# Gated scan and MoE on one core: another order of the head, h by units, and a table of shifted due times

## The chip, the cores and the metric

The program runs on one core of a Trainium2 chip. A core has five engines that run their own instruction queues in order and wait for each other through semaphores: TensorE (PE, matmuls), VectorE (DVE), ScalarE (ACT), GpSimd (POOL) and SyncE (SP, which here issues most of the DMA transfers). The metric is the device time of one execution in microseconds (us); lower is better.

## The reference

Two stages follow each other. The first is a gated linear recurrence over 768 tokens for 4 batches and 8 heads of 48 channels, the second a feed-forward layer over the 3072 tokens that come out of it.

```python
mag = np.sqrt(a_re * a_re + a_im * a_im)
scale = np.minimum(mag, 0.999) / (mag + 1e-06)
a_re_n, a_im_n = (a_re * scale, a_im * scale)
for t in range(S):
    ar, ai = (a_re_n[:, :, t, :, None], a_im_n[:, :, t, :, None])
    new_re = ar * S_re - ai * S_im
    new_im = ar * S_im + ai * S_re
    kv = np.einsum('bhd,bhe->bhde', k[:, :, t], v[:, :, t])
    S_re, S_im = (new_re + kv, new_im)
    y[:, :, t] = np.einsum('bhd,bhde->bhe', q[:, :, t], S_re)
...
h = x @ w_in                       # 3072x384 @ 384x2048
g = np.where(pos, h, np.where(neg, 0.0, (h + beta) ** 2 / (4.0 * beta)))
return (g @ w_out).astype(np.float32)   # 3072x2048 @ 2048x384
```

## The kernel before

The recurrence is computed without a loop over time. A complex gate is a decay and an angle; the running sums of both over the tokens turn the recurrence into masked attention between k and q that have been scaled by exponentials and by a sine and a cosine. The 3072 tokens are 12 units of 256 tokens. For each unit u, `gates(u)` makes the scaled k and q and `attend(u)` the attention:

- `gates(u)` first takes logarithms and exponentials of the gates (the first table of ACT, `natural_log_exp_and_others`), normalises, and for units 0 and 1 forms the running sum of the decay with matmuls against a triangular matrix (tile `o`, line 693). From that sum ACT makes two exponentials (line 747, into tile `x`), and DVE multiplies k and q (tile `kq`, one tile for both) by them (line 761). `yield` ends this part. The second part begins with a load of ACT's other table (`trig_and_small`, left out for unit 1, which shares unit 0's load), takes the arctangent, sums the angles with matmuls again, reduces them to turns (lines 773 and 781), takes sine and cosine (all plain ACT functions stand in line 644), and multiplies `kq` by each (`turn`, line 854: the product with the cosine goes into tile `x`, the one with the sine back into `kq`).
- `spread` moves these products into tiles `hd`, in which a head's 96 rows lie together: five DMAs for each product, ten for each unit, all issued by SP at line 434. In a packed tile `hd` the even rows come from one product and the odd rows from the other.
- `attend(u)` works on two chunks of 128 tokens. PE makes scores (line 1010) and transposes (950); DVE copies the scores under a causal mask (tile `am`, 1022), ACT copies the transposes (tile `kT`, 956); PE then adds the values (1054 with the state, 1062 with `am`) and the products for the state (979). The result goes to tile `xr`, and six small DMAs move the rest of its rows (`xr<-xr`).

`moe(blk)` is the feed-forward layer on a block of two units, 512 tokens, so there are six blocks. `split` casts `xr` to a rounded part `xH` (ACT) and the rest `xL` (DVE). For each of 16 slices f of the hidden layer `gemm1` accumulates nine matmuls of 512 columns into a PSUM tile `h` (there are two of them, in turn), ACT and DVE make g out of it (1212 to 1249; tile `g`, then its rounded part `gh` and the rest `gl`), and `gemm2` adds nine matmuls into three tiles `o` (line 1263) that last for the whole block. A tile `h` is free again when DVE has read it at line 1231. In block 0 two more steps of g are on ACT instead of DVE.

The weights are 16 packed loads (`raw_i`, `raw_o`). Each is decoded by three DVE instructions (464, 473, 482) and a cast on ACT (488) into `wi` or `wo`; its low part is made by PE and ACT for the first five loads (`rest`, 502, 503, 517) and by DVE (493) for the others. Slice f of the hidden layer needs loads `i` and `o` number f // 2.

Nothing is issued in the order in which it is written. Each operation goes into a `Plan` with an engine, a cost and what it depends on; `Plan.order` gives every operation a due time, backwards from the due times of the matmuls, and then schedules greedily: the engine that is free first takes the operation with the earliest due time among those whose inputs it takes to be ready. `emit` writes the instructions in that order and fills planned gaps of PE with idle matmuls (line 1326), up to the first matmul of `gemm1`. `NUDGE` is a table from the number of an operation to nanoseconds that are added to its due time.

Of the kernel before, what the change touches and what calls it, by code (L numbers as in the profile page):

```python
# [15 lines left out]
AF = mybir.ActivationFunctionType  # L16
# [3 lines left out]
P = 128  # L20
# [8 lines left out]
NJ = DM // P  # L29
NF = DFF // P  # L30
CH = 128
HC = CH // 2
U = 256
# [3 lines left out]
BLOCKS = ((0, 1), (2, 3), (4, 5), (6, 7), (8, 9), (10, 11))  # L37
# [25 lines left out]
MOVE_FIX, MOVE_ISSUE = 1750, 605  # L63
LOAD = 410.0
AHEAD, LATER, LATER_MOVE = 3000, 2000, 250
NUDGE = {}
MOVE = {16: 180, 32: 185, 128: 360, 288: 1330}
TABLE = 1294
FIRST = 66000
# [1 line left out]
LAG = 3  # L71
# [236 lines left out]
def per(n):  # L308
    return n / 2.4 + 14
# [23 lines left out]
def gated_scan_moe(  # L333
# [54 lines left out]
    pl = Plan()  # L388
# [28 lines left out]
    weight = {}  # L417
    seen = {}
    kinds = {}
# [7 lines left out]
    V_, A_, PE_ = nc.vector, nc.scalar, nc.tensor  # L427
# [15 lines left out]
    def table(name):  # L443
        pl.op("ACT", TABLE, lambda: nc.scalar.preload_act_table_set(name), w=[TAB])
# [160 lines left out]
    def gates(u):  # L605
# [32 lines left out]
        def ac(out, src, f, r, w, tab=False, **kw):  # L638
            acc_ = kw.get("accum_out")
            cost = act(N, ptr=not isinstance(kw.get("bias", 0.0), float), acc=acc_ is not None)  # L640
            (pl.op if acc_ is None else mark)(
                "ACT",
                cost,
                lambda: A_.activation(out(), src(), f, **kw),  # L644
                r=[*r] + ([TAB] if tab else []),
                w=w,
            )
# [31 lines left out]
        )  # L679
        js = ((0, 2), (2, 3))  # L680

        def running(src, part_, slots, name):

            out = []
            for (j0, j1), slot in zip(js, slots):
                R = tl(slot, [P, j1 - j0, U], F32, f"{name}_{u}_{j0}", ps)

                def run(R=R, j0=j0, j1=j1):
                    x = src().rearrange("p j t -> p (j t)")
                    for j in range(j0, j1):  # L690
                        for c in range(NC):
                            k = c * DM + j * P
                            PE_.matmul(
                                R.get()[:, j - j0, c * CH :],
                                x[:, k : k + P],
                                sums.rearrange("p c t -> p (c t)")[:, : U - c * CH],
                                start=c == 0,
                                stop=c == NC - 1,
                            )

                kinds[
                    pl.op("PE", (j1 - j0) * (pe32(U) + pe32(CH)), run, r=[part_], w=[R])
                ] = "sum"
                out.append(R)
            return out
# [55 lines left out]
        ve(dve(2 * N), lambda: V_.tensor_tensor(KQ.get(), KQ.get(), X.get(), op=ALU.mult), [X], [KQ])  # L761

        yield
        if u != 1:
            table("trig_and_small")
        ac(I, I, AF.Arctan, [], [i], True)
        c = 1.0 / (2 * math.pi)
        if by_token:
            for (j0, j1), R in zip(js, running(I, i, TOKEN[u], "turns")):
# [127 lines left out]
                        w=[(h, (e, 1 + q))],  # L897
                    )

        turn(X, 0)  # L900
        for g in range(3):
            spread(g, 0, X)
        turn(KQ, 1)
        for g in range(3):
            spread(g, 1, KQ)
        if u == 1:
            moved.append(len(pl.ops) - 1)

# [263 lines left out]
    def moe(blk):  # L1172
# [6 lines left out]

        def gemm1(f):  # L1180
            H = tl(turn_of("h", 2), [P, T], F32, f"h_{blk}_{f}", ps)
            for j in range(NJ):

                def mms(j=j):
                    sl = slice(j * P, (j + 1) * P)
                    for n, (part, x) in enumerate(((0, XH), (1, XH), (0, XL))):
                        PE_.matmul(  # L1187
                            H.get(),
                            weight["i", f // 2].get()[:, f % 2, part, sl],
                            x.get()[:, j, :],  # L1190
                            start=j == 0 and n == 0,
                            stop=j == NJ - 1 and n == 2,
                        )

                kinds[len(pl.ops)] = "moe"
                pl.op(
                    "PE",
                    3 * per(T),
                    mms,
                    r=[weight["i", f // 2]] + [(x, (ub, j)) for x in (XH, XL) for ub in range(len(BLOCKS[blk]))],  # L1200
                    w=[H],
                    due=t0 + STEP * (f + j / 6 - 0.6 * (f + 1 == NF and held_back > 0)),
                )
            SS = tl(turn_of("s", 3), [P, T], F32, f"s_{blk}_{f}")
            G = tl(turn_of("s", 3), [P, T], F32, f"g_{blk}_{f}")
            GH = tl(turn_of("gg", 6), [P, T], F32R, f"gh_{blk}_{f}")
            GL = tl(turn_of("gg", 6), [P, T], F32R, f"gl_{blk}_{f}")
            spare = blk < SPARE
            pl.op(
                "ACT",  # L1210
                act(T, ptr=True, psum=True),
                lambda: A_.activation(  # L1212
                    SS.get(), H.get(), AF.Relu, bias=c_half, scale=-0.5 if spare else 0.5
                ),
                r=[H],
                w=[SS],
            )
            if spare:
                pl.op(
                    "ACT",  # L1220
                    act(T, ptr=True),
                    lambda: A_.activation(SS.get(), SS.get(), AF.Relu, bias=c_one, scale=-1.0),
                    w=[SS],
                )
                pl.op(
                    "ACT", act(T), lambda: A_.activation(SS.get(), SS.get(), AF.Square), w=[SS]
                )
            pl.op(
                "DVE",
                dve(T),  # L1230
                lambda: V_.tensor_tensor(G.get(), H.get(), SS.get(), op=ALU.max),  # L1231
                r=[H, SS],
                w=[G],
            )
            if not spare:
                pl.op(
                    "DVE",
                    dve(T),
                    lambda: V_.scalar_tensor_tensor(  # L1239
                        G.get(), SS.get(), 1.0, G.get(), op0=ALU.min, op1=ALU.mult  # L1240
                    ),
                    r=[SS],
                    w=[G],
                )
            pl.op("ACT", act(T), lambda: A_.copy(GH.get(), G.get()), r=[G], w=[GH])  # L1245
            i = pl.op(
                "DVE",
                dve(T),
                lambda: V_.tensor_tensor(GL.get(), G.get(), GH.get().bitcast(F32), op=ALU.subtract),  # L1249
                r=[G, GH],  # L1250
                w=[GL],
            )
            gs[f] = (GH, GL)
            gated.append(i)
# [24 lines left out]

        held_back = BACK if blk == NBLK - 1 else 0  # L1280
        for k in range(NF + LAG):
            if k < NF:
                gemm1(k)
            if LAG <= k < NF + LAG - held_back:
                gemm2(k - LAG)
        for m in range(NJ if held_back else 0):
            for f in range(NF - held_back, NF):
                gemm2(f, (m,), NF - f - 1 + (m * held_back + f) / 9)
# [48 lines left out]
    first, second = gates(0), gates(1)  # L1337
    next(first)
    next(second)
    list(first)  # L1340
    attend(0)
    list(second)
# [300 lines left out]
```

## Time and profile before

| | |
|---|---|
| time, median of 3 runs | 573.28 us (572.74 to 575.54) |
| time of the profiled execution | 574.38 us |
| its span, first to last instruction | 572.6 us |
| PE busy | 558.9 us (98%), of it idle matmuls 27.3 us |
| DVE busy | 439.8 us (77%) |
| ACT busy | 391.2 us (68%) |
| granted TensorE clock, mean | 0.997 of full speed |

The profiled execution's time is 1.8 us longer than its span; that part lies around the first and the last instruction. The busy shares are means over the whole span, in which the first 76 us (gates and attention of units 0 and 1, the first weights, the first two slices) are another regime than the rest.

### The profile page before, as it was taken

The page shows a single profiled execution, that of the slowest core. Times are in us where ns is not written, and L with a number is a line of the kernel's source. Part 1 is how long each engine was busy: PE and PEld are TensorE (multiplying, and loading weights), DVE is VectorE, ACT ScalarE, POOL GpSimd, SP SyncE. Part 2 cuts the span into 40 slices and gives each one's busy share as a digit, 9 for nine tenths or more (in the row PEclk, how much of TensorE's full clock was granted, in tenths as well). Part 3 has the DMA queues.
Part 4 walks back from the last instruction along what each step waited for, and adds up shares of the span by engine and source line. Part 5 has one row for each costly group of instructions (what it writes and reads, how often), then busy time and mean ns, then how long its engine had stood idle before and what let it go on. Part 6 is the DMA issues. An engine that isn't in the chain of part 4 may idle for free.

```text
span 572.6 us, 10735 instructions
## 1 busy us (share of the span) xinstructions
PE 558.9 (98%) x4288; PEld 465.5 (81%) x4288; DVE 439.8 (77%) x611; ACT 391.2 (68%) x636; POOL 4.1 (1%) x27
## 2 busy tenths in 40 slices
PE   8999989999999999999999999999999999999996
PEld 8788868888888888888888888888888888888884
DVE  7998999989969988887797887987766555454562
ACT  7787688989975757757657686666455453369972
POOL 2000000000000000000000000000000000000000
PEclk9999999999999999999999999999999999999998
DMA  8848483663541512614403414402543500087811
GB/s 349 339 130 275 135 284 100 183 217 113 165 158 46 179 46 71 199 57 109 160 3 96 174 56 109 161 2 75 194 167 98 172 1 8 20 311 271 281 55 60
DMA packets 23686, 80.57 MB, mean 141 GB/s; under 512 B 4560, under 2 KB 10320, under 8 KB 23632
## 3 DMA queue, kind: packets, MB, share of 16 engines
q1 hardware_dynamic: 23488, 79.71, 42.1%
q8 instruction: 35, 0.57, 0.4%
q14 instruction: 19, 0.16, 0.1%
q10 hardware_dynamic: 144, 0.13, 0.1%
HBM read 55.05 MB, written 4.72 MB: 104 GB/s over the span
## 4 chain that ended last, share of the span: by engine, by line
PE 90%; DVE 3%; ACT 2%; DMA 2%; issue 1%; SPq 1%; POOL 0%; ACTq 0%; POOLq 0%; DVEq 0%
PE o L1263 35%; PE h L1187 34%; PE at L1010 6%; PE at L1062 3%; PE at L1054 3%; PE idle L1326 3%; PE at L979 3%; PE at L950 2%; DMA out_dram<-ob 1%; DVE kq L761 1%; ACT ai L644 1%; ACT x L747 1%; SPq L434 1%; DMA xr<-xr 1%; DVE ai L781 0%
## 5 line engine op out<-in xcount | busy, mean ns | idle before, releaser
L1187 PE MATMUL h<-xH,wi 128*128 128x512 f32 x576 | 181.3, 396 | 2.9 <-DVE g L1231 2.9
L1263 PE MATMUL o<-gh,wo 128*128 128x512 f32 x576 | 180.3, 394 | 0.0
L1187 PEld LDWEIGHTS h<-xH,wi 128*128 128x128 f32 x576 | 105.4, 188 | 25.0 <-DVE g L1231 3.5
L1263 PEld LDWEIGHTS o<-gh,wo 128*128 128x128 f32 x576 | 106.3, 188 | 22.8 <-issue 0.7
L1187 PE MATMUL h<-xL,wi 128*128 128x512 f32 x288 | 112.5, 391 | 0.4 <-DVE xL L1164 0.4
L1263 PE MATMUL o<-gl,wo 128*128 128x512 f32 x288 | 112.4, 390 | 0.0
L1231 DVE TENSOR_TENSOR g<-h,s 128x512 f32<-128x512 f32 x96 | 65.9, 687 | 54.4 <-ACT s L1212 53.6
L1212 ACT ACTIVATE s<-h,cst 128x512 f32<-128x512 f32 x96 | 65.8, 685 | 47.5 <-PE h L1187 46.6
L1245 ACT CAST gh<-g 128x512 fp32r<-128x512 f32 x96 | 59.3, 618 | 55.9 <-DVE g L1239 48.6
L1249 DVE TENSOR_TENSOR gl<-g,gh 128x512 fp32r<-128x512 f32 x96 | 65.8, 685 | 32.8 <-ACT gh L1245 30.8
L1187 PEld LDWEIGHTS h<-xL,wi 128*128 128x128 f32 x288 | 54.1, 188 | 12.7 <-DVE xL L1164 1.2
L1263 PEld LDWEIGHTS o<-gl,wo 128*128 128x128 f32 x288 | 54.1, 188 | 11.8 <-DVE gl L1249 0.3
L1239 DVE SCALAR_TENSOR_TENSOR g<-s,g 128x512 f32<-128x512 f32 x80 | 55.3, 691 | 2.2
L644 ACT ACTIVATE ai<-ai 128x768 f32<-128x768 f32 x48 | 40.4, 845 | 10.1 <-DVE ai L797 5.3
L1010 PEld LDWEIGHTS at<-hd 96*64 96x64 f32 x704 | 32.5, 137 | 7.6 <-issue 5.9
L1010 PE MATMUL at<-hd 96*64 96x64 f32 (+1 forms) x704 | 36.7, 251 | 0.0
L1022 DVE COPY_PREDICATED am<-tri,at 128x512 f32<-128x512 uint32 x44 | 32.1, 743 | 5.1 <-PE at L1010 4.2
L719 DVE TENSOR_TENSOR_SCAN ai<-again,ai 128x768 f32<-128x768 uint8 x20 | 35.1, 1753 | 0.4
L1062 PE MATMUL at<-am,V 128*64 128x128 f32 x352 | 32.9, 273 | 0.0
L1054 PE MATMUL at<-hd,st 96*64 96x128 f32 x304 | 30.5, 278 | 0.0
L1326 PE MATMUL idle<-tri,ident 128*128 128x128 f32 x208 | 27.3, 291 | 1.8 <-POOL tri masks.py:66 1.8
L1326 PEld LDWEIGHTS idle<-tri,ident 128*128 128x128 f32 x208 | 26.5, 206 | 2.8 <-POOL tri masks.py:66 1.8
(127 smaller groups left out, 642.5 us busy)
## 6 DMA issues: line engine op xcount, KB each, us to landing
chk<-in_wl_dram SPq DMA_DIRECT2D x16, 768.0 KB, 6.5
kq<-in_kq_dram SPq DMA_DIRECT2D x12, 768.0 KB, 6.0
ai<-in_ari_dram SPq DMA_DIRECT2D x10, 768.0 KB, 6.7
V<-in_v_dram SPq DMA_DIRECT2D x12, 576.0 KB, 4.1
hd<-x SPq DMA_DIRECT2D x24, 288.0 KB, 3.2
hd<-kq SPq DMA_DIRECT2D x24, 288.0 KB, 4.3
raw_i<-in_wl_dram SPq DMA_DIRECT2D x8, 768.0 KB, 6.9
raw_o<-in_wl_dram SPq DMA_DIRECT2D x8, 768.0 KB, 5.0
```

The source lines that it names most:

```text
L644: lambda: A_.activation(out(), src(), f, **kw),
L1010: PE_.matmul(SC.get()[o : o + HC, i + e, HC * k :], t[:, 0, ks], t[:, 1, qs], start=True, stop=True,)
L1054: PE_.matmul(o_, st.get().rearrange("p h e -> p (h e)")[:, lo : lo + 64], head(h)[:, 1, cs], start=True, stop=False,)
L1062: PE_.matmul(o_, V.get()[:, c, lo : lo + 64], ams[pr // 2].get()[:, 2 * (pr % 2) + e, :], start=st is None, stop=True,)
L1187: PE_.matmul(H.get(), weight["i", f // 2].get()[:, f % 2, part, sl], x.get()[:, j, :], start=j == 0 and n == 0, stop=j == NJ - 1 and n == 2,)
L1212: lambda: A_.activation(SS.get(), H.get(), AF.Relu, bias=c_half, scale=-0.5 if spare else 0.5),
L1231: lambda: V_.tensor_tensor(G.get(), H.get(), SS.get(), op=ALU.max),
L1239: lambda: V_.scalar_tensor_tensor(G.get(), SS.get(), 1.0, G.get(), op0=ALU.min, op1=ALU.mult),
L1245: pl.op("ACT", act(T), lambda: A_.copy(GH.get(), G.get()), r=[G], w=[GH])
L1249: lambda: V_.tensor_tensor(GL.get(), G.get(), GH.get().bitcast(F32), op=ALU.subtract),
L1263: PE_.matmul(PO[m].get(), weight["o", f // 2].get()[:, f % 2, part, sl], g.get(), start=f == 0 and n == 0, stop=f == NF - 1 and n == 2,)
L1326: PE_.matmul(idle["h1"], ident, mask, start=True, stop=True)
```

## The change

Five edits. (1) The generators of the two first units are advanced by turns: unit 0 up to its second table, then a load of that table, the arctangents of both units, a load of the first table for unit 1's exponentials, and a load of the second table again for the sines. (2) For units 0 and 1 the product with the sine comes first and goes into tile `x`, and the one with the cosine goes back into `kq`; for the other units nothing changes here. (3) In block 0 the slices f = 0 and 1 of `gemm1` run as two sets of nine matmuls with 256 columns, one for each unit. (4) `gemm2` is written ahead of `gemm1` of the same step. (5) `NUDGE` gets 195 entries.

```diff
-NUDGE = {}
+NUDGE = {
+    25: -59700, 43: 11500, 46: -22300, 58: -180800, 68: -10500, 74: -12000, 75: -16200,
...
+}
+HALVES = 2
...
+        def arctan():
+            ac(I, I, AF.Arctan, [], [i], True)
+
+        yield
+        if u == 1:
+            arctan()
+            yield
...
         yield
+        if u > 1:
+            table("trig_and_small")
         if u != 1:
-            table("trig_and_small")
-        ac(I, I, AF.Arctan, [], [i], True)
+            arctan()
+            yield
...
-        turn(X, 0)
-        for g in range(3):
-            spread(g, 0, X)
-        turn(KQ, 1)
-        for g in range(3):
-            spread(g, 1, KQ)
+        for t, e in ((X, 1), (KQ, 0)) if by_token else ((X, 0), (KQ, 1)):
+            turn(t, e)
+            for g in range(3):
+                spread(g, e, t)
...
         def gemm1(f):
             H = tl(turn_of("h", 2), [P, T], F32, f"h_{blk}_{f}", ps)
...
+            halves = blk == 0 and f < HALVES
+            for n, (lo, hi) in enumerate(((0, U), (U, T)) if halves else ((0, T),)):
+                ubs = (n,) if halves else range(len(BLOCKS[blk]))
+                for j in range(NJ):
...
+                    done = pl.op(
+                        "PE",
+                        3 * per(hi - lo),
+                        mms,
+                        after=[done] if n and not j else (),
+                        r=[weight["i", f // 2]] + [(x, (ub, j)) for x in (XH, XL) for ub in ubs],
+                        w=[(H, n)],
+                        due=t0 + STEP * (f + j / 6 - 0.6 * (f + 1 == NF and held_back > 0)),
+                    )
...
         for k in range(NF + LAG):
+            if LAG <= k < NF + LAG - held_back:
+                gemm2(k - LAG)
             if k < NF:
                 gemm1(k)
-            if LAG <= k < NF + LAG - held_back:
-                gemm2(k - LAG)
...
     next(first)
     next(second)
+    next(first)
+    table("trig_and_small")
+    next(first)
+    next(second)
+    table("natural_log_exp_and_others")
+    next(second)
+    table("trig_and_small")
     list(first)
```

What this does to the order shows at three places. ACT before, from the exponentials of unit 1's running sum (`x_156<-o`; unit 0's tiles are `ai_132` and `x_151`, unit 1's `ai_134` and `x_156`) over the table load and the two arctangents (`ai_132<-ai_132`, `ai_134<-ai_134`) to unit 0's sine, the first of the last row's two instructions:

```order
L747 ACTIVATE x_156<-o_112 128x2x256 x2
L747 ACTIVATE x_156<-o_113 128x256 x2
L517 CAST wi_252<-rest_i_0_257 128x384
L444 ACT_TABLE_LOAD
L517 CAST wi_252<-rest_i_1_272 128x384
L644 ACTIVATE ai_132<-ai_132 128x768
L644 ACTIVATE ai_134<-ai_134 128x768
L488 CAST wo_292<-raw_o_143 128x2x384
L488 CAST wi_304<-raw_i_147 128x2x384
L517 CAST wo_292<-rest_o_0_301 128x384
L644 ACTIVATE ai_132<-ai_132 128x768 x2
```

The same stretch of ACT in the changed kernel (unit 1's tiles are now `ai_135` and `x_161`), from the last exponentials of unit 0 to the sine, `ai_132<-ai_132` behind the third load, and the two casts after it:

```order
L674 ACTIVATE x_161<-x_161,cst 128x3x256
L785 ACTIVATE x_151<-o_113 128x256
L474 ACT_TABLE_LOAD
L674 ACTIVATE ai_132<-ai_132 128x768
L674 ACTIVATE ai_135<-ai_135 128x768
L474 ACT_TABLE_LOAD
L785 ACTIVATE x_161<-o_112 128x2x256 x2
L785 ACTIVATE x_161<-o_113 128x256 x2
L474 ACT_TABLE_LOAD
L674 ACTIVATE ai_132<-ai_132 128x768
L518 CAST wi_291<-raw_i_137 128x2x384
L518 CAST wi_294<-raw_i_139 128x2x384
```

The casts of weights have moved behind the sine, and three loads of a table stand there instead of one. On SP, before, the ten moves of unit 0 stand in this order, cosine product `x` and sine product `kq` in turns, with two loads of weights just ahead:

```order
L449 DMA raw_o_248<-in_wl_dram 128x1536
L449 DMA raw_i_276<-in_wl_dram 128x1536
L434 DMA hd_0_346<-x_151 48x1536
L434 DMA hd_1_349<-x_151 48x1536
L434 DMA hd_2_353<-x_151 32x1024
L434 DMA hd_0_346<-kq_139 48x1536
L434 DMA hd_1_349<-kq_139 48x1536
L434 DMA hd_2_353<-kq_139 32x1024
L434 DMA hd_2_353<-x_151 16x512 x2
L434 DMA hd_2_353<-kq_139 16x512 x2
```

And on SP in the changed kernel, where `x` is the sine product:

```order
L479 DMA raw_i_157<-in_wl_dram 128x1536
L464 DMA hd_1_306<-x_151 48x1536
L464 DMA hd_0_316<-x_151 48x1536
L464 DMA hd_2_321<-x_151 32x1024
L464 DMA hd_2_321<-x_151 16x512 x2
L464 DMA hd_0_316<-kq_141 48x1536
L464 DMA hd_1_306<-kq_141 48x1536
L464 DMA hd_2_321<-kq_141 32x1024
L464 DMA hd_2_321<-kq_141 16x512 x2
```

All five moves of `x` are now ahead of those of `kq`, and the two last loads of weights have gone behind all twenty moves of both units. The third place is DVE from the first g of block 0 (`g_0`) on, before:

```order
L1231 TENSOR_TENSOR g_0_801<-h_0_749,s_0_785 128x512
L665 SCALAR_TENSOR_TENSOR x_727<-ai_525,x_727 128x3x256
L1249 TENSOR_TENSOR gl_0_822<-g_0_801,gh_0_808 128x512
L1231 TENSOR_TENSOR g_1_834<-h_1_757,s_1_794 128x512
L1022 COPY_PREDICATED am_82<-tri,at_109 128x512
L493 TENSOR_TENSOR wi_824<-raw_i_492,wi_824 128x2x384
```

And after it:

```order
L1273 TENSOR_TENSOR g_0_774<-h_0_716,s_0_757 128x512
L503 SCALAR_TENSOR_TENSOR raw_o_711<-raw_o_711,y_o_770 128x768
L1273 TENSOR_TENSOR g_1_787<-h_1_690,s_1_762 128x512
L1291 TENSOR_TENSOR gl_0_792<-g_0_774,gh_0_783 128x512
L512 SCALAR_TENSOR_TENSOR raw_o_711<-raw_o_711 128x768
L1291 TENSOR_TENSOR gl_1_808<-g_1_787,gh_1_797 128x512
```

Decoding of weights that stood ahead of `g_0` now stands behind it. From `g_0` to block 0's last `gl` DVE has 104 instructions before and 109 after: seven of weights (two of line 473, two of 482, one each of 464, the low part of an `i` and of an `o`) and one of the state (line 991) have come in, and three of `xL` have gone behind. On PE, idle matmuls fall from 104 to 77, and behind the first matmul of `h` the stretches of feed-forward matmuls are broken by attention 51 times instead of 56.

## Rows read from the trace of the kernel before

**Rows 1.** Stretches of PE: us, busy (instructions), granted clock, DMA share, GB/s.

```profile
76.03:567.00 490.97, 490.75 (x3600) 1.00 0.38 125
...
569.70:570.00 0.30, 0.00 (x0) 0.50 0.19 34
```

**Rows 2.** Timeline of PE: start, us, line, tiles, count, idle before and its releaser.

```profile
34.01 6.86 PE L1326 MATMUL idle<-tri,ident 128*128 128x128 f32 x60
...
41.80 1.72 PE L1010 MATMUL at<-hd 96*64 96x128 f32 x32
...
76.03 0.74 PE L1187 MATMUL h<-xH,wi 128*128 128x512 f32 x2 [2.73 <-DVE g L1231]
```

**Rows 3.** Timeline of ACT: unit 0's first exponential, the table load, unit 0's sine.

```profile
15.61 0.60 ACT L747 ACTIVATE x<-o 128x512 f32<-128x512 f32 x1 [0.83 <-PE o L693]
...
21.37 1.28 ACT L444 ACT_TABLE_LOAD   x1
22.67 0.48 ACT L517 CAST wi<-rest_i 128x384 fp32r<-128x384 f32 x1
...
28.70 1.72 ACT L644 ACTIVATE ai<-ai 128x768 f32<-128x768 f32 x2 [0.50 <-DVE ai L781]
```

**Rows 4.** Groups of ACT from 13 to 34 us, columns as on the page.

```profile
L644 ACT ACTIVATE ai<-ai 128x768 f32<-128x768 f32 x6 | 5.0, 844 | 1.3 <-DVE state L806 0.6 <-DVE ai L781 0.5
...
L747 ACT ACTIVATE x<-o 128x512 f32<-128x512 f32 x4 | 2.3, 596 | 1.1 <-PE o L693 0.8 <-DVE state L736 0.2
L747 ACT ACTIVATE x<-o 128x256 f32<-128x256 f32 x4 | 1.4, 386 | 0.5 <-DVE state L736 0.5
```

**Rows 5.** Timeline of DVE in block 0: a low part, a decoding step, two `xL`.

```profile
128.47 0.95 DVE L493 TENSOR_TENSOR wo<-raw_o,wo 128x768 fp32r<-128x768 f32 x1
129.34 0.55 DVE L464 TENSOR_SCALAR y_i<-raw_i 128x768 uint32<-128x768 uint32 x1
129.81 0.68 DVE L1231 TENSOR_TENSOR g<-h,s 128x512 f32<-128x512 f32 x1
...
156.18 0.75 DVE L1164 TENSOR_TENSOR xL<-xr,xH 128x256 fp32r<-128x256 f32 x2
156.85 0.68 DVE L1249 TENSOR_TENSOR gl<-g,gh 128x512 fp32r<-128x512 f32 x1
```

**Rows 6.** Timeline of DVE in the head: a product, the first mask copy, a wait.

```profile
31.68 1.76 DVE L854 TENSOR_TENSOR x<-kq,ai 128x1536 f32<-128x1536 f32 x1
...
43.68 1.34 DVE L1022 COPY_PREDICATED am<-tri,at 128x512 f32<-128x512 uint32 x2
...
53.97 0.56 DVE L464 TENSOR_SCALAR y_o<-raw_o 128x768 uint32<-128x768 uint32 x1 [2.09 <-DMA raw_o<-in_wl_dram]
```

**Rows 7.** Timeline of SP: issues of unit 0's first moves.

```profile
33.47 1.86 SPq L434 DMA_DIRECT2D hd<-x  x3
35.43 2.21 SPq L434 DMA_DIRECT2D hd<-kq  x3
```

**Rows 8.** DMA issues from 35.4 to 37.65 and 33 to 35.4: KB, us to landing.

```profile
hd<-kq SPq DMA_DIRECT2D x2, 288.0 KB, 5.6
...
hd<-x SPq DMA_DIRECT2D x2, 288.0 KB, 3.7
```

**Rows 9.** Stretches of DVE, columns as in the first group: from the first mask copy, from g_0.

```profile
43.68:75.97 32.29, 29.27 (x40) 1.00 0.67 205
75.97:157.45 81.48, 77.71 (x105) 1.00 0.55 175
```

**Rows 10.** Timeline of PE: the first matmuls behind scores, and block 0's end.

```profile
131.11 0.73 PE L1187 MATMUL h<-xH,wi 128*128 128x512 f32 x2
131.68 0.39 PE L1187 MATMUL h<-xL,wi 128*128 128x512 f32 x1
...
157.35 0.62 PE L1263 MATMUL o<-gh,wo 128*128 128x512 f32 x2
157.81 0.39 PE L1263 MATMUL o<-gl,wo 128*128 128x512 f32 x1
```

More of the change, by code (lines that the diff above doesn't have):

```diff
@@ L1181, in gemm1, with mms @@
             H = tl(turn_of("h", 2), [P, T], F32, f"h_{blk}_{f}", ps)
[L1182 to L1203, printed above, removed]
+            halves = blk == 0 and f < HALVES
+            for n, (lo, hi) in enumerate(((0, U), (U, T)) if halves else ((0, T),)):
+                ubs = (n,) if halves else range(len(BLOCKS[blk]))
+                for j in range(NJ):
+                    def mms(j=j, lo=lo, hi=hi):
+                        sl = slice(j * P, (j + 1) * P)
+                        for n, (part, x) in enumerate(((0, XH), (1, XH), (0, XL))):
+                            PE_.matmul(
+                                H.get()[:, lo:hi],
+                                weight["i", f // 2].get()[:, f % 2, part, sl],
+                                x.get()[:, j, lo:hi],
+                                start=j == 0 and n == 0,
+                                stop=j == NJ - 1 and n == 2,
+                            )
+                    kinds[len(pl.ops)] = "moe"
+                    done = pl.op(
[6 more added lines that the diff above has]
+                        due=t0 + STEP * (f + j / 6 - 0.6 * (f + 1 == NF and held_back > 0)),
+                    )
             SS = tl(turn_of("s", 3), [P, T], F32, f"s_{blk}_{f}")
```

27 rows, old and new, of the table NUDGE are left out of this document.

## The prediction

> **What bounds the kernel now.** I read the page first, then stretches of PE, then the timelines of the first 76 us engine by engine, then DVE's stretches. The table above says that PE is busy for 98% of the span; the reader should see where that is useful work. From the third slice of block 0 at 76.03 us to the last matmul PE has 490.75 busy of 490.97 us [rows 1]: it is the limit there, and its time changes only if its instructions change or if something begins to make it wait. Ahead of that point PE is filled with idle matmuls, 6.86 us of them before unit 0's scores, and it waits 2.73 us before that third slice for DVE's g_0, which frees the PSUM tile [rows 2]. So the end is set by when g_0 is done, just ahead of 76.03, by PE's 491 us behind it, and by an unchanged tail of 5.6 us (572.6 less 567.0).
>
> **The head, step by step.** Unit 0's exponentials start at 15.61 us, and its sine at 28.70, when DVE has the turns [rows 3]. In the new order ACT first makes unit 0's four exponentials with one of unit 1 in between. The start moves little, since unit 0's chain is only placed ahead of unit 1's: I take 15.2. Two exponentials of 0.6 us, two of 0.4 and a plain function of 0.84 [rows 4] make 2.8 us; with a short wait for DVE's copy, 18.1. A table load takes 1.3 us from its start to the next instruction [rows 3]. So load, two arctangents (1.7), load, unit 1's four exponentials (2.0) and load end at 25.7. DVE has less ahead of unit 0's turns: one weight (three instructions, 0.5 + 0.9 + 0.9 from start to start), the last third of another [rows 5], and one product of 1.76 [rows 6], 5 us in all. Not all of it helps, because DVE must wait for the exponentials to scale k and q; adding up its queue in the new order from 15.2 on gives the turns at 25.7 too. The sine then starts at 25.8, 2.9 us sooner. The first product no longer waits for the cosine but for the sine, and follows it by 3.2 us (one plain function, DVE's product, two hand-overs): SP's first issue goes from 33.47 [rows 7] to 29.0. Behind the sine two casts of weights of the same 768 columns (1.7) and the absolute value stand ahead of the cosine, which ends at about 30.6; the second product ends at 32.4. These casts cost nothing as long as SP still issues `x`: three issues take 1.86 us [rows 7], so five last to 32.1. If they were longer they would move the second product one for one.
>
> The scores start 6.4 us after the second product's first issue now (35.43 to 41.80), with 5.6 us from issue to landing while `x` is still in flight, against 3.7 us for the first moves [rows 2, 7, 8]. In the new order `x` has had 3.4 us alone, so I take 4.8 us, between 4.3 (3.7 and one more issue) and 6.2 (5.6 and one more): scores at 37.2 instead of 41.80. The first mask copy, 1.9 us behind the scores' start, is at 39.2 instead of 43.68 [rows 6], 4.5 us sooner, 3.1 to 5.0 by these ends. From there to the end of g_0 at 75.97 DVE needs the same work in both orders, 29.27 us, and loses 3.02 us [rows 9], of which 2.09 on a load of weights [rows 6]; that load is now issued right behind the moves, some 6 us sooner. I give back half of that wait: g_0 ends at 70.4, **5.5 us sooner**; with none of it back and late landing 3.1, with all of it and early landing 7.1.
>
> The halves of slices 0 and 1 are inside that number. Eighteen matmuls of 256 columns move into the wait for unit 1's moves, where idle matmuls stood; the other eighteen replace eighteen of 512 columns at 0.23 us [rows 10]. Half the columns cost from 0.12 us (half the time) to 0.23 us (no gain) each, so 2.1 to 4.1 us instead of 4.1. Either way it is over before g_0, which hangs on DVE's queue; without that cover it would be worth up to 2 us.
>
> **PE's own work behind it.** Where feed-forward matmuls follow scores, the first two take 0.57 us from start to start instead of 0.46 [rows 10]. I price every change from the one kind to the other at these 0.11 us. With 51 stretches instead of 56, two changes into attention and five out of it are gone: **0.8 us less**. Nothing to twice that are the ends, since the row shows two matmuls and not what lies around them.
>
> **What DVE is owed.** The work that leaves the head comes back. Between g_0 and block 0's last `gl` DVE has seven weight instructions and one state update more and three `xL` less. From start to start a long weight instruction takes 0.87 us, a short one 0.47 (the state update I take as a short one), two `xL` of 256 columns 0.67 and one of 768 as long as a low part of that size [rows 5]: 6 x 0.87 + 0.47 + 0.47 - 0.67 - 0.87 = 4.6 us more. This stretch is 81.48 us with 77.71 busy [rows 9], that is 3.8 us lost to waits, and PE reaches that `gl` only 0.3 us after it is made (157.81 against 156.85 + 0.68) [rows 5, 10]. PE's work in between is the same. So PE must wait 4.6 - 3.8 - 0.3 = 0.5 us plus whatever DVE still loses: 0.5 us if it never waits, 4.3 us if it loses as much as now. The new order interleaves DVE's chains more, so I take 1.7 us lost: **2.2 us given back**. Further on it costs nothing more: DVE's share falls and each slice's g is made many us ahead.
>
> The other edits have one answer: writing `gemm2` ahead of `gemm1` and the due times act only through the order counted above, and the tail's order is the same from slice 12 of the last block on.
>
> **Sum.** -5.5 - 0.8 + 2.2 = -4.1 us against the profiled execution's own 574.38 us, which is 1.1 us above the median shown: 570.3 on its scale, 569.2 us on the median's.
>
> **A rule against the change.** By the rows a switch of table costs 1.3 us, and the cast behind it starts at once [rows 3]; the two added loads are 2.6 us of ACT, in the chain above. The Trainium skill, "ScalarE: Activation LUTs", section "What ACT_TABLE_LOAD costs", puts a switch at about 2.66 us, a load of 1.28 us and a drain of about the same length, and its rules for kernel authors ask to do all of one set before switching. By that the two added loads would cost 5.3 us and the gain of the head would be some 2.7 us less; the trace has the load's length as stated and no drain behind it, so I go by the trace.
>
> **The rivals**, each on the median's scale. *DVE's debt is paid in full.* DVE loses 3.8 us in block 0 as now, so PE waits 4.3 us: -5.5 - 0.8 + 4.3 = -2.0, 571.3 us. For it: DVE stands at 95% there. Against it: its waits were harmless so far and nothing ordered them away. *TensorE's clock falls.* The granted clock is at half (0.50, the 1.2 GHz level) in the stretch from 569.70 us, 2.7 us after the last matmul, but at 1.0 through the stretches that follow the 2.73 us wait before 76.03 [rows 1, 2]. In the new order only ten idle instructions (five idle matmuls), 1.1 us by the sixty of 6.86, stand between the last work at about 32.2 and the scores at 37.2, a wait of some 4 us. If the clock falls there, unit 0's first scores and values, 4 to 5 us of PE, take up to 2.3 us more, and the gain shrinks to 1.8: 571.5 us. The skill's page "TensorE: Matmul & The Clock Gate" says in its part 1 that the throttled clock is the default and that only activity releases it, which speaks for this. *Nothing moves.* Scores wait for something other than the moves, as a weight's cast: the head gains nothing, but work has also not left DVE's early queue: about 573 us. *Slower.* DVE becomes the limit of block 0: each us that it loses there beyond 1.7 is a us of PE, so from 5.8 us lost (0.5 + 5.8 eats the 6.3) the kernel is no faster, and from 8.7 us it is slower by 0.5%. The head shows that DVE can lose 2.09 us to one load, but block 0 loses 3.8 in all now; at 10 us it would be 577.5 us. *Better.* Early landing, all of the 2.09 us back and DVE almost without waits: -7.1 - 0.8 + 0.8 = -7.1, 566.2 us.
>
> **How the numbers follow.** A difference under 0.5% (2.9 us) can't be told from none in these measurements. Forecast, 567.4 to 570.6: 0.45. Better than that: 0.21. DVE's debt or the clock, 570.6 to 573: 0.23. Nothing: 0.04. Slower than before: 0.07, most of it by over 0.5%. Faster by over 0.5% holds the forecast, the better case and a small part of the rivals' low ends: 0.68. Same: 0.26. Slower by over 0.5%: 0.06. The range leaves out one in ten at each end: 565.0 to 572.6 us.
>
> **What would show it.** In the profile after: unit 0's sine at 25 to 26.5 us; the first `hd<-x` issue near 29 and the scores near 37; g_0 done near 70.5; PE waits for DVE in block 0 (on `g`, `gl` or a weight) of about 2 us in sum, where there were none; no waits behind it; table loads with no gap behind them. The forecast is wrong if scores start after 39, if the clock falls before them, or if PE's waits in block 0 pass 4 us.

## The result, and the profile after

| | before | changed |
|---|---|---|
| time, median of 8 runs each | 574.85 us (572.74 to 576.82) | 569.68 us (567.77 to 571.05) |
| ratio | | 0.991, 95% interval 0.989 to 0.994 |
| time and span of the profiled execution | 574.38, 572.6 us | 570.26, 568.5 us |
| mean granted clock of the profiled execution | 0.997 | 0.992 |

The kernel is 0.9% faster; 0.7% (569.2 against 573.28 us) was forecast. By the medians that is 5.2 us. Between the two profiled executions the difference is 4.1 us, as the sum had it, but it is put together in another way.

The stretches of PE in the changed kernel, from the end of slice 1 of block 0 (us, busy and instructions, granted clock, DMA share, GB/s):

```profile
65.90:69.24 3.34, 0.00 (x0) 0.75 0.86 255
69.24:74.50 5.26, 5.26 (x13) 0.51 0.60 150
74.50:563.00 488.50, 488.03 (x3589) 1.00 0.39 128
```

Against [rows 1] PE's work from slice 2 on begins 6.8 us sooner (69.24 for 76.03) and ends only 4.0 sooner. The reason stands in the middle line: the granted clock, which was 1.0 through the wait before 76.03, falls within the wait before 69.24 (0.75 in the mean there) and is at half, the 1.2 GHz level, for nearly all of the next 5.26 us. The timeline of PE shows the same from the matmuls (line 1048 makes scores, 1228 is `gemm1`, 1305 `gemm2` in the changed kernel):

```profile
36.45 1.56 PE L1048 MATMUL at<-hd 96*64 96x128 f32 x32
...
69.24 1.22 PE L1228 MATMUL h<-xH,wi 128*128 128x512 f32 x2 [3.35 <-DVE g L1273]
70.26 0.63 PE L1228 MATMUL h<-xL,wi 128*128 128x512 f32 x1
...
74.49 0.63 PE L1305 MATMUL o<-gh,wo 128*128 128x512 f32 x2
...
151.94 0.50 PE L1305 MATMUL o<-gh,wo 128*128 128x512 f32 x1 [0.15 <-DVE wo L523]
154.81 0.50 PE L1305 MATMUL o<-gl,wo 128*128 128x512 f32 x1 [0.27 <-DVE gl L1291]
```

The wait for g_0 is still there and has grown from 2.73 [rows 2] to 3.35 us. Behind it twelve matmuls last from 69.24 to 74.49, 5.25 us, where twelve cost 12 x 0.23 = 2.8 at [rows 10]. The two waits for DVE in block 0 are 0.4 us together as listed. Of the head, ACT's timeline from unit 0's first exponential to its sine:

```profile
14.64 1.08 ACT L785 ACTIVATE x<-o 128x512 f32<-128x512 f32 x2 [1.21 <-PE o L731]
...
17.51 1.28 ACT L474 ACT_TABLE_LOAD   x1
18.81 1.58 ACT L674 ACTIVATE ai<-ai 128x768 f32<-128x768 f32 x2
20.41 1.28 ACT L474 ACT_TABLE_LOAD   x1
21.70 1.83 ACT L785 ACTIVATE x<-o 128x512 f32<-128x512 f32 x4
23.55 1.28 ACT L474 ACT_TABLE_LOAD   x1
24.89 0.84 ACT L674 ACTIVATE ai<-ai 128x768 f32<-128x768 f32 x1
```

Each of the three loads takes 1.3 us from its start to the next instruction, as in [rows 3]. (The Trainium skill, "ScalarE: Activation LUTs", section "What ACT_TABLE_LOAD costs", has a drain of about the length of a load with each switch; none of the three shows one.) SP's moves of unit 0 follow:

```profile
28.15 3.31 SPq L464 DMA_DIRECT2D hd<-x  x5
31.56 3.21 SPq L464 DMA_DIRECT2D hd<-kq  x5
```

And DVE, in stretches from the first mask copy to g_0 and from g_0 to block 0's last `gl`:

```profile
37.65:69.19 31.54, 29.31 (x41) 0.97 0.66 219
69.19:154.76 85.57, 81.69 (x110) 0.97 0.53 173
```

The first line answers to 32.29 us with 29.27 busy [rows 9]: the same work, 0.8 us less lost. The second has 4.0 us more work than [rows 9] and loses 3.9 us, as much as before. Where it loses them DVE's timeline tells:

```profile
75.63 0.69 DVE L1273 TENSOR_TENSOR g<-h,s 128x512 f32<-128x512 f32 x1 [1.57 <-ACT s L1268]
77.58 0.74 DVE L1060 COPY_PREDICATED am<-tri,at 128x512 f32<-128x512 uint32 x1 [1.26 <-PE at L1048]
...
114.43 0.56 DVE L494 TENSOR_SCALAR y_i<-raw_i 128x768 uint32<-128x768 uint32 x1 [0.88 <-DMA raw_i<-in_wl_dram]
```

2.8 of the 3.9 us are waits right behind the stretch of low clock, for what PE and then ACT make.

### The profile page after: what moved, and what is told of

It reads as the page before. It is cut to its first block, busy times and chain, and to the rows that moved or that the text cites. A ratio compares the mean times of both kernels' runs of the same rounds, so it can differ in the third digit from the quotient of the medians.

```text
span 568.5 us, 10701 instructions
## 1 busy us (share of the span) xinstructions
PE 555.3 (98%) x4252; PEld 462.0 (81%) x4252; DVE 439.1 (77%) x611; ACT 394.9 (69%) x638; POOL 4.1 (1%) x27
## 4 chain that ended last, share of the span: by engine, by line
PE 78%; DVE 12%; ACT 5%; issue 2%; DMA 1%; POOL 0%; DVEq 0%; ACTq 0%; POOLq 0%
PE h L1228 31%; PE o L1305 30%; PE at L1048 5%; PE idle L1368 3%; PE at L1092 3%; PE at L1100 3%; PE at L1017 2%; PE at L988 2%; DVE ai L757 1%; ACT ai L674 1%; DMA raw_i<-in_wl_dram 1%; DVE am L1060 1%; DVE kq L799 1%; PE o L731 1%; DVE kq L894 1%
## 5 line engine op out<-in xcount | busy, mean ns | idle before, releaser
L1228 PE MATMUL h<-xH,wi 128*128 128x512 f32 (+1 forms) x588 | 184.6, 396 | 3.9 <-DVE g L1273 3.4
L1228 PEld LDWEIGHTS h<-xH,wi 128*128 128x128 f32 x588 | 107.7, 190 | 27.5 <-DVE g L1273 4.5
L1228 PE MATMUL h<-xL,wi 128*128 128x512 f32 (+1 forms) x294 | 114.5, 389 | 0.1
L1228 PEld LDWEIGHTS h<-xL,wi 128*128 128x128 f32 x294 | 55.8, 190 | 12.0 <-DVE xL L1202 0.3
L1048 PE MATMUL at<-hd 96*64 96x128 f32 (+1 forms) x704 | 35.8, 250 | 0.0
L994 ACT COPY kT<-at 128x384 f32<-128x384 f32 x36 | 15.9, 480 | 15.5 <-PE at L988 15.2
```

Of the source, the lines that this page charges most:

```text
L1048: PE_.matmul(SC.get()[o : o + HC, i + e, HC * k :], t[:, 0, ks], t[:, 1, qs], start=True, stop=True,)
L1228: PE_.matmul(H.get()[:, lo:hi], weight["i", f // 2].get()[:, f % 2, part, sl], x.get()[:, j, lo:hi], start=j == 0 and n == 0, stop=j == NJ ...
```

## The experiments

Two theories stood behind the trace. Theory A: DVE sets the end of block 0 (PE takes the last `gl` the moment it is ready, at 154.81), and the low clock only makes PE arrive later at work that isn't ready sooner. Theory B: the low clock is a loss of its own. In the same runs stood the question what each edit of the change is worth. Where a run is said to be some us longer or shorter than another, that is the difference of their ratios times 574 us.

**Idle matmuls in the wait for g_0** (`a_fill`). `at1` is a PSUM bank that is free there.

```diff
         def gemm1(f):
+            if blk == 0 and f == 2:
+                fill["op"] = len(pl.ops)
...
+    FILL = 12
...
+        if "over" in idle and i == fill["op"]:
+            for _ in range(FILL):
+                PE_.matmul(banks["at1"][:, :P], ident, mask, start=True, stop=True)
```

> The changed kernel with 12 more idle matmuls (24 instructions, about 2.7 us) behind slice 1 of block 0, in the 3.35 us in which PE waits for g_0. The granted clock should then stay at 1.0 and slices 2 and 3 take 2.8 us instead of 5.3. Theory A, DVE's queue sets the end of block 0: PE only arrives 2.5 us sooner at work that DVE hands over late, so PE's waits for DVE in block 0 rise from 0.4 to about 2.7 us and the time stays within 0.4 us of the changed kernel's (ratio to the kernel before about 0.991). Theory B, the low clock is a loss of its own: the time falls by 2.5 us (ratio about 0.987) and the waits in block 0 stay under 1 us.

Measured: ratio 0.988 (0.986 to 0.991), 1.8 us less than the changed kernel; the two intervals overlap by 0.002, so the traces must say which theory holds. PE's stretches and timeline in this run:

```profile
66.00:69.04 3.04, 2.36 (x23) 1.00 0.91 271
69.04:72.00 2.96, 2.96 (x13) 1.00 0.90 216
72.00:559.60 487.60, 487.25 (x3589) 1.00 0.39 128
```

```profile
65.52 2.84 PE L1375 MATMUL at<-tri,ident 128*128 128x128 f32 x24
69.04 0.73 PE L1231 MATMUL h<-xH,wi 128*128 128x512 f32 x2 [0.68 <-DVE g L1276]
...
71.90 0.62 PE L1308 MATMUL o<-gh,wo 128*128 128x512 f32 x2
...
151.23 0.50 PE L1308 MATMUL o<-gl,wo 128*128 128x512 f32 x1 [0.27 <-DVE gl L1294]
```

The clock stays at 1.0, the twelve matmuls take 2.86 us (69.04 to 71.90), and the wait for the last `gl` is still 0.27 us, where theory A wanted waits of 2.7: theory B holds and theory A falls. DVE's stretches say why:

```profile
37.47:68.98 31.51, 29.28 (x41) 1.00 0.68 221
68.98:151.60 82.62, 82.03 (x112) 1.00 0.54 179
```

With the clock up DVE loses 0.6 us between g_0 and the end of block 0 instead of 3.9. The waits that I had read as DVE's own were made by the slow PE.

How often the clock falls is seen from the mean clock of each execution. Of the eight runs of the changed kernel five were at 0.992 or 0.993 (569.18 to 571.05 us, mean 570.3) and three at 0.996 (567.77 to 569.09, mean 568.6); all six with the idle matmuls were at 0.997 or more (566.43 to 568.57). So the profiled execution shows the commoner case. The three are no clean opposite: the eleven profiles here in which the clock falls only behind the last matmul read 0.997 to 0.999, so these three may have lost some clock too; no profile shows where.

**The same in the kernel before** (`b_fill`): the same edit, with 10 such matmuls ahead of its slice 2.

```diff
+    FILL = 10
```

> The kernel before with 10 more idle matmuls (about 2.2 us) in its own 2.73 us wait for g_0, where the clock stayed at 1.0. Both theories: no change, ratio 0.999 to 1.001. If it is faster, the wait before slice 2 costs something that the granted clock does not show.

Measured: 0.999 (0.997 to 1.001), no difference that can be told. Yet of the 23 runs of the kernel before that were timed beside it, ten had a mean clock of 0.993 to 0.996 (mean time 575.4 us) and 13 of 0.997 or more (573.8), and all twelve with the idle matmuls were at 0.997 or more. It loses clock in some executions too; where in them, its one profile, at 0.997, doesn't show.

**Four low parts on GpSimd** (`a_relief`), to take work from DVE in block 0; and with the idle matmuls too (`a_both`).

```diff
-                lambda: V_.tensor_tensor(lo(), yf(), hi().bitcast(F32), op=ALU.subtract),
+                lambda: (nc.gpsimd if n in (8, 10, 12, 14) else V_).tensor_tensor(lo(), yf(), hi().bitcast(F32), op=ALU.subtract),
```

> The changed kernel with four low parts of o weights (loads 3 to 6) made by GpSimd instead of DVE, in the same place of the order: DVE has 4 x 0.87 = 3.5 us less to do between g_0 and block 0's last gl. The low clock stays. Theory A: only the two waits in block 0 go (0.4 us), since PE, slowed by 2.5 us, is just in step with DVE; ratio about 0.990. Theory B: the same 0.4 us. A loss would mean that GpSimd is too slow for these parts or slows DVE down.

> Both edits together: idle matmuls in the wait for g_0, and four low parts on GpSimd. Theory A: now PE neither runs slow nor waits for DVE, so the two edits give together what neither gives alone, 2.5 + 0.4 = 2.9 us less than the changed kernel (ratio about 0.986). Theory B: the same 2.9 us, but 2.5 of it already with the idle matmuls alone. Either way this would beat both kernels, if GpSimd keeps up.

Measured: 0.997 (0.995 to 0.999) and 0.993 (0.990 to 0.995): 3.2 us longer than without GpSimd in the first case and 2.5 in the second. The loss that the expectation named came. GpSimd's timeline and DVE's at the first and the last of the four parts:

```profile
96.41 2.27 POOL L523 TENSOR_TENSOR wo<-raw_o,wo 128x768 fp32r<-128x768 f32 x1 [91.50 <-ACT wo L518]
...
146.23 2.15 POOL L523 TENSOR_TENSOR wo<-raw_o,wo 128x768 fp32r<-128x768 f32 x1 [17.71 <-ACT wo L518]
```

```profile
96.85 2.25 DVE L494 TENSOR_SCALAR y_i<-raw_i 128x768 uint32<-128x768 uint32 x1
...
146.69 2.52 DVE L512 SCALAR_TENSOR_TENSOR raw_o<-raw_o 128x768 uint32<-128x768 uint32 x1
```

A part takes GpSimd 1.9 to 2.3 us where DVE needs 0.95, and the DVE instruction that starts within it takes 2.25 instead of 0.55 us [rows 5] and ends 0.4 us behind GpSimd's: it stood still until GpSimd was through. The Trainium skill, "SBUF — State Buffer", section "SBUF: two separate sides", says that DVE and GpSimd share a pair of ports under an exclusive lock that is held for a whole instruction (of DVE's, those in a two-port mode or with two inputs in SBUF); the rows agree. At all four parts it is so: instructions of 0.55, 0.55, 0.55 and 0.96 us take 2.25, 1.98, 2.16 and 2.52, 6.3 us lost for the 3.5 taken off. So these runs don't relieve DVE.

Yet `a_relief` bears on the clock, since its PE meets the same wait without idle matmuls. In its profiled execution the clock stayed at 1.0 through that wait and behind it:

```profile
69.80 0.74 PE L1228 MATMUL h<-xH,wi 128*128 128x512 f32 x2 [3.36 <-DVE g L1273]
```

Of its twelve runs three had a mean clock of 0.996 to 0.998 (mean time 571.0 us) and nine of 0.992 to 0.995 (572.9). So, as far as mean clocks tell, a wait of this length costs the clock in some executions of a program and not in others, and within one program the low clock goes with 1.9 us more, as theory B has it.

**The two added table loads taken away** (`f_noload`). Unit 1's sums and exponentials go ahead of the first load, in the written order only, and two loads fall away; idle matmuls as in `a_fill`. The edit, shortened to its sense:

```diff
         order = self.order()
+        # sums and exponentials of unit 1, then the load and both arctangents, at one place
+        move = sums_1 + exponentials_1 + load + arctan_0 + arctan_1
+        rest = [i for i in order if i not in {*move, *two_other_loads}]
+        at = max(rest.index(i) for i in inputs_of(move)) + 1
+        order = rest[:at] + move + rest[at:]
```

> The changed kernel with the 12 idle matmuls, and with unit 1's four exponentials (and the PE sums that they need) put ahead of the first load of the second table, so that the two other loads fall away. Nothing else moves. Theory: unit 0's sine now waits for unit 1's sums and exponentials, it starts near 27.6 us instead of 24.9, and as the head sets g_0 and g_0 the end, the time is 2.3 to 2.8 us longer than with the idle matmuls alone (ratio 0.992 to 0.993). Rival: the two loads cost as much as they bring, or the moves wait for something else; no change (0.988).

Measured: 1.000 (0.999 to 1.001), that is 6.5 us longer than `a_fill`, and the whole gain of the change gone. Its ACT timeline, SP's and PE's:

```profile
24.10 1.28 ACT L485 ACT_TABLE_LOAD   x1
25.39 1.57 ACT L686 ACTIVATE ai<-ai 128x768 f32<-128x768 f32 x2
30.95 0.85 ACT L686 ACTIVATE ai<-ai 128x768 f32<-128x768 f32 x1 [3.98 <-DVE ai L836]
```

```profile
34.19 3.32 SPq L475 DMA_DIRECT2D hd<-x  x5
```

```profile
75.44 0.74 PE L1246 MATMUL h<-xH,wi 128*128 128x512 f32 x2 [0.68 <-DVE g L1291]
```

The sine comes 6.1 us later than in the changed kernel (30.95 for 24.89), the first issue 6.0 (34.19 for 28.15), slice 2 6.4 later than in `a_fill`: the delay of the sine is carried through to slice 2, as the theory said. The end is 6.5 us later by the ratios and 7.8 in the two profiled executions, where 1.1 us are lost behind slice 2, most of it at one wait for ACT. The size was more than twice what I expected, since unit 1's sums and exponentials wait for others on PE and DVE once they stand ahead. A planner free to arrange the rest might do better than this, which no run tried; so 6.5 us is at most what the loads bring. In five of these twelve runs the mean clock was 0.994 to 0.996 in spite of the idle matmuls; the profile, at 0.998, doesn't show where they lost it.

**Cosine first** (`f_cos`, with the table of due times and idle matmuls).

```diff
-        for t, e in ((X, 1), (KQ, 0)) if by_token else ((X, 0), (KQ, 1)):
+        for t, e in ((X, 0), (KQ, 1)):
```

> The changed kernel with the 12 idle matmuls, and with the product with the cosine first again for units 0 and 1. Theory: the first move is issued behind the cosine, near 30.5 us instead of 28.1, the second product's landing and the scores come 1.5 to 3 us later, and the time grows by as much (ratio 0.991 to 0.993). Rival: only the second product's landing counts, and it is ready as early as now: less than 1 us (0.988 to 0.990).

Measured: 1.026 (1.024 to 1.027), 15 us longer than the kernel before. Neither expectation: against `a_fill` the first issue is 1.2 us later and slice 2 3.1 us, but then one row of PE's timeline alone costs more than that:

```profile
109.93 0.80 PE L1308 MATMUL o<-gl,wo 128*128 128x512 f32 x1 [9.82 <-DVE gl L1294]
```

The clock falls in this wait and stays at half to 114 us, and it falls once more at 186, behind a wait of 1.87 us. The due times are shifts for the operations of one order. With other edges between the operations the planner makes an order out of them in which a `gl` comes 9.8 us late; without the table the same swap costs 1.1 us (`n_cos`, below). So the run tells what the table is worth to another kernel, and not what the sine is worth.

**An empty table** (`f_nonudge`, with idle matmuls), and on top of it cosine first (`n_cos`), which asks the question anew.

```diff
-NUDGE = {
-    25: -59700, 43: 11500, 46: -22300, 58: -180800, 68: -10500, 74: -12000, 75: -16200,
...
-}
+NUDGE = {}
```

> The changed kernel with the 12 idle matmuls and an empty table of shifted due times: the planner's own order for the other four edits. Theory: the head's gain (table order, sine first) is in the generators and stays, so most of the 6.8 us remain, and the table is worth 1 to 3 us through the order of DVE's work around g_0 (ratio 0.990 to 0.994). Rival: the table carries the change, and without it the time is that of the kernel before (0.998 to 1.004).

> The planner's own order (empty table, 12 idle matmuls) with the cosine's product first, against the run with the empty table and the sine's product first (0.9935). Theory: the first issue comes some 2 us later (about 30 us instead of 28.1), the scores 1 to 2 us later than their 39.4, ratio 0.995 to 0.997. Rival: the order of the two products is worth nothing by itself in the planner's own order, 0.993 to 0.994, and the 21 us of the earlier run came from the table of due times not fitting another order.

Measured: 0.9935 (0.992 to 0.995) without the table, 0.9955 (0.994 to 0.998) with the cosine first as well. PE's timeline in the first, then in the second:

```profile
39.44 1.56 PE L1020 MATMUL at<-hd 96*64 96x128 f32 x32
...
65.84 0.50 PE L1202 MATMUL h<-xH,wi 128*128 128x256 f32 x2 [1.55 <-ACT xH L1167]
...
68.64 0.58 PE L1202 MATMUL h<-xL,wi 128*128 128x256 f32 x1
...
72.86 0.71 PE L1202 MATMUL h<-xH,wi 128*128 128x512 f32 x2
```

```profile
40.55 1.56 PE L1020 MATMUL at<-hd 96*64 96x128 f32 x32
...
74.22 0.72 PE L1202 MATMUL h<-xH,wi 128*128 128x512 f32 x2 [0.68 <-DVE g L1247]
```

The table is worth 3.0 us by the ratios, and not the whole change. In the profiled executions slice 2 starts 3.8 us later without it (72.86 against 69.04) and the end comes 4.1 later, so nearly all of it lies ahead of slice 2. The sine first brings slice 2 1.4 us forward; the two ratios differ by 1.1 us, but their intervals overlap. The first execution also shows the clock falling where the idle matmuls don't reach: less than 2 us after PE has gone back to work behind a wait of 1.55 us, the granted clock goes to half (0.50 from 68 to 70 us) and a matmul of 256 columns takes 0.58 us instead of 0.28.

**Slices 0 and 1 in one set each** (`a_merged`, without idle matmuls; `m_fill`, with nine).

```diff
                         sl = slice(j * P, (j + 1) * P)
+                        if halves:
+                            if not lo:
+                                return
+                            lo = 0
```

> The changed kernel (without more idle matmuls) with slices 0 and 1 of block 0 in one set of nine matmuls of 512 columns each, at the place of the second half. Theory: g_0 hangs on DVE's queue and not on these matmuls, so g_0 and the time stay (ratio 0.989 to 0.991), and the wait ahead of slice 2 gets shorter, from 3.4 to about 2.8 us, so that the clock falls in fewer executions. Rival: the halves bring time of their own, up to 2 us (0.993 to 0.995).

> The changed kernel with slices 0 and 1 in one set each and 9 idle matmuls behind them. If the low clock was all that the halves cost, the two remedies do not add up: the same as either alone, ratio 0.987 to 0.988. If the halves cost more than the clock: below 0.986.

Measured: 0.9876 (0.986 to 0.989) and 0.987 (0.985 to 0.989). The first is 2.1 us shorter than the changed kernel and as short as the one with idle matmuls; both remedies together give no more. PE's waits in `a_merged` (total us, times, longest):

```profile
PE h L1232 <- DVE g L1277: 2.8, 1, 2.8
```

The halves bring nothing, as both expectations for the theory had it, and they take something: with them PE is done sooner, waits 3.35 instead of 2.8 us, and loses clock in most executions; without them the mean clock was 0.997 or 0.998 in all four. That the length of the wait makes the difference is likely and not shown: `a_relief` kept the clock behind 3.36 us, and `f_nonudge` and `f_cos` lost it behind 1.55 and 1.87. Either remedy beats the kernel before. Against the changed kernel the intervals touch or overlap, by 0.002 at most; that all three runs with a remedy come out at 0.987 to 0.988 is what the gain rests on.

**Four low parts computed twice on DVE**, in the changed kernel (`f_double`) and in the one before (`b_double`), both with idle matmuls. This measures what DVE's debt costs.

```diff
-                lambda: V_.tensor_tensor(lo(), yf(), hi().bitcast(F32), op=ALU.subtract),
+                lambda: [
+                    V_.tensor_tensor(lo(), yf(), hi().bitcast(F32), op=ALU.subtract)
+                    for _ in range(2 if n in (8, 10, 12, 14) else 1)
+                ],
```

> The changed kernel with the 12 idle matmuls, and with four low parts of o weights (loads 3 to 6) computed twice on DVE, the second time over the first: 4 x 0.87 = 3.5 us more for DVE between g_0 and block 0's last gl. By the way of reckoning of the prediction (that gl is now used as soon as it is made, and DVE loses only about 0.5 us in between) all of it becomes a wait of PE: waits of PE in block 0 rise from 0.3 to 3.3 to 3.8 us, time +3.0 to +3.5 (ratio 0.993 to 0.994). Rival: DVE has slack that the waits do not show, less than 1.5 us.

> The kernel before with idle matmuls in its wait for g_0, and the same four low parts twice. There the last gl of block 0 is ready 0.3 us ahead of its use, and DVE loses 3.8 us to waits. If these waits are slack that more work fills up (as the prediction reckoned for the changed kernel): PE waits 0 to 1 us, ratio 0.999 to 1.001. If they stay where they are (a load that lands late, a scan's input): 3.2 us, ratio 1.004 to 1.005.

Measured: 0.994 (0.993 to 0.996) and 1.002 (1.001 to 1.003), that is 3.6 us more than `a_fill` and 2.0 us more than `b_fill`, for 3.5 us of work. PE's timeline in `f_double`:

```profile
101.90 0.73 PE L1234 MATMUL h<-xH,wi 128*128 128x512 f32 x2 [0.47 <-DVE g L1279]
...
129.53 0.73 PE L1234 MATMUL h<-xH,wi 128*128 128x512 f32 x2 [0.98 <-DVE g L1279]
...
148.52 0.50 PE L1311 MATMUL o<-gh,wo 128*128 128x512 f32 x1 [0.63 <-DVE wo L524]
...
156.00 0.50 PE L1311 MATMUL o<-gl,wo 128*128 128x512 f32 x1 [0.27 <-DVE gl L1297]
```

In the changed kernel DVE has no slack left in block 0, and the work reaches the end in full: counted from the start of slice 2 and against the same matmuls of `a_fill`, PE is 4.0 us late at the end of block 0 in this execution. The first three waits in the rows make up 2.1 of it (`a_fill` has the last one too), shorter ones the rest. In the kernel before, by the ratios, 1.5 of 3.5 us went into slack and into waits that were harmless, and 2.0 became time; in its profile one wait for `g`, 1.74 us at 151.40, is most of that.

## Why the prediction was right

The time lay within the range and near the number. The mechanism was right (g_0 sooner, PE's 491 us shifted with it), but in the profiled execution three terms of the sum were off and cancelled each other, so that 4.1 came out for 4.1 is luck:

| us against the kernel before | forecast | changed, profiled | with idle matmuls |
|---|---|---|---|
| slice 2 starts (g_0) | -5.5 | -6.8 | -7.0 |
| low clock behind it | 0 | +2.4 | 0 |
| PE waits for DVE in block 0 | +2.2 | +1.2 | +0.3 |
| the rest of PE's work from slice 2 on | -0.8 | -0.8 | -0.7 |
| tail | 0 | -0.1 | -0.4 |
| sum | -4.1 | -4.1 | -7.8 |

The low clock and the waits of the changed kernel are read against the run with idle matmuls, whose PE does the same 3600 matmuls in the same order from slice 2 on. Counted from the start of slice 2 the same matmul starts 2.39 us later at 74.49 and 3.3 us later from the end of block 0 on; the 0.9 us between lie at single matmuls of block 0 that wait for `g`, `gl` or `wo`, partly too short for a wait to be listed, and come on top of the 0.3 us listed in the other run. The fourth row is what is left between slice 2's start and the end of PE's work in each run (567.0, 563.0 and 559.6).

- **The head.** Each step came in the forecast order and some 0.8 us ahead of it: sine 24.89 (25.8 forecast), first issue 28.15 (29.0), second product 31.56 (32.4), scores 36.45 (37.2), g_0 some 1.2 us sooner than 70.4. 0.6 us of that is the chain's start (14.64, not 15.2), which lay between 14.2 and 15.4 in the profiles of the runs that keep the table. The landing was sized right, 4.9 us for 4.8. The mask copy follows the scores by 1.2 us and not by 1.9, a distance which I had carried over from before without asking what filled it. Of the 2.09 us of waiting for a load half was reckoned to come back; DVE lost 0.8 us less.
- **The casts and the added loads cost what was said**, and `f_noload` shows that the order of the tables carries the head. That ACT's two extra loads lie in the chain and still pay is the point of the change that was right against the rule.
- **TensorE's clock** was a rival with a wrong place. I looked for the fall ahead of unit 0's scores, because few idle matmuls were left there; but PE has low parts of weights to make in that stretch, and the clock stays up. It fell in the wait before slice 2, the very wait in [rows 2] whose cover I counted as free: I let the halves move eighteen matmuls and said "either way it is over before g_0". That was so, and the wait that it left, 3.35 us for 2.73, is the one in which the clock fell. The price was near, up to 2.3 us forecast for a fall and 2.4 measured. The step that failed is the term that I put at nothing for that wait, on the strength of the 1.0 read from one execution of the kernel before, which loses clock in ten of 23 runs itself.
- **DVE's debt** was mis-sized, 2.2 us for 1.2, and for 0.3 with the clock up. The work came near what was counted (4.0 us more for 4.6); DVE loses 0.6 us instead of the 1.7 that I took, once the clock is up, and the planner's order stays even with PE. `f_double` confirms the reckoning by which each further us would have been a us of PE.
- **Switches.** PE's own work behind slice 2 is 0.7 to 0.8 us shorter, as forecast; that it is the switches was not tried by itself.
- **The halves** are worth nothing, as forecast, and the **table** acts through the order alone, worth 3.0 us here. `gemm2` written ahead of `gemm1` was not tried by itself.

## What to carry to other kernels

When a change makes a bottleneck engine's input arrive sooner, ask of every wait that is left what it does to the clock: a wait that cost nothing but its own length can cost the speed of what comes behind, in some executions of the same program and not in others. Filling it with idle matmuls, or not splitting the work in front of it, kept the clock behind that wait here; it doesn't reach other waits. A table of shifts tuned for one order belongs to that order alone, and one profiled execution shows one of the cases that the runs contain.

## What the runs showed of the hardware

- The granted clock fell in a wait of PE of 3.35 us in the profiled execution, and five of eight runs had a mean clock as low as that one's; a wait of 2.8 us in `a_merged` cost no clock in four runs. The fall cost 2.4 us, since the twelve matmuls behind the wait ran at the 1.2 GHz level.
- The length of one wait doesn't settle it: a wait of 3.36 us in `a_relief` left the clock at 1.0, and it fell behind waits of 1.55 us (`f_nonudge`) and 1.87 us (`f_cos`), after PE had gone back to work.
- A GpSimd tensor_tensor of 768 columns took 1.9 to 2.3 us, and the DVE instruction that started within it stood still until it ended, four times out of four (2.25 us for 0.55 at the first).
- Loads of ACT's table that start about 3 us after each other cost 1.3 us each and nothing more (17.51, 20.41 and 23.55 us).
